# Splitting the 128-row products of an attention and feed-forward kernel over the two halves of TensorE's rows

## The chip, the cores and the metric

The kernel runs on one core of a Trainium2 chip. The metric is the device time of one execution, in microseconds (us); the times of several runs are given by their median. One execution is also recorded by the hardware profiler, and its trace gives the start and the duration of each instruction on each engine.

The engines are TensorE (PE in the profile; its weight loads are PEld), VectorE (DVE), ScalarE (ACT), GpSimd (POOL), and SyncE (SP), which here only issues transfers. TensorE multiplies a stationary operand (the weights, up to 128 rows by 128 columns) with a moving one, and writes or adds the result into a bank of PSUM. The rows are the contracted dimension. A product that contracts over only 64 rows can sit on the lower or the upper half of the rows. In the names used here, T0 is the half of rows 0 to 63 and T1 that of rows 64 to 127.

## What is computed

A block-sparse attention over 4 batches and 8 heads of 768 positions with 64 numbers each, and then a feed-forward layer of 512 to 1024 to 512 with a SoLU and a layer norm, on 3072 tokens:

```python
scores = scale * np.matmul(q, k.transpose(0, 1, 3, 2))
# mask: neighbouring blocks of 32, first and last block, three sampled blocks
scores = np.where(mask, scores, -1000000000.0)
attn = np.exp(scores - max); attn = attn / attn.sum()
x = np.matmul(attn, v)           # heads side by side: 3072 x 512
h = x @ w_in                     # 3072 x 1024
e = np.exp(h - max); solu = h * e / e.sum()
ln = (solu - mean) / np.sqrt(var + 1e-6) * g_ln
out = ln @ w_out                 # 3072 x 512, float32
```

## The kernel before

**Passes and units.** The 768 queries of a batch are taken 256 at a time, so there are 12 passes (four batches by three). A pass has 12 units: four pairs of heads by three parts of the keys (256 keys each). There are 144 units. A unit s does the following:
- `scores(s)`: for two heads and two chunks of 128 keys, the scores are built transposed (keys on the partitions) in a PSUM tile of two banks, `sco`, one bank for each head. There are two such tiles. Each head contracts over 64 rows, head 0 on T0 and head 1 on T1, so the eight products of a unit (four of K times Q, four that add the mask) are 64 rows by 256 columns and come in pairs, T0 and T1 in turn.
- `exps(s)`: one exponential of ScalarE over the 128 x 1024 scores gives `exs`.
- `outs(s)`: eight products with `exs` as weights and the values `VA` (64 numbers and a one, so 65 columns) as the moving operand, contracted over 128 keys, add into `op`. After the third unit of a pair of heads, `normalise` divides by the sum in `op` and writes `xb`.

**The layer.** A pass of 256 queries gives two tiles of 128 tokens. Their x is turned by a transposing transfer (`x_turn`; in the first and the last pass by TensorE). `h_mms` makes h in two PSUM banks: for each half of the 1024 columns four products of 128 rows by 512 columns. `e_exp` takes the exponential of the whole tile on ScalarE, with the sum; `solu` multiplies on VectorE; `ln_turn` turns the result by a transfer; `stats` and `rstd` make the factor of the norm; `o_mms` adds eight products of 128 rows by 512 columns into the one bank `o`, and `store` scales that and sends it out.

**The order.** Nothing is ordered by the compiler. Each step is put on a list with a time in units, `at(when, function, ...)`; the list is sorted by that time (ties in the order of listing), and each engine gets its instructions in this order. So these times set an order, not a clock. A unit s has its exponential at s, the scores of s+2 at s+0.8 and its `outs` at s plus `PV[u]`, u being the part of the keys. `layer_h` and `layer_o` put the layer of a pass into the pass after it and the one after that: h of a tile begins at hs, which is 5 or 11 units into the next pass, and o at hs+9. E = 144 is the end of the last unit and L the number of the last pass; the layer of the last two passes is listed by hand around E, and what is listed after E forms the tail: the x turn of pass L (`x_turn_pe`, at E+0.2), then its h, exponentials, turns, o and stores. Transfers of q, k and v for the next batch are issued on SP from `LD` units apart; GpSimd casts them to bf16, and SP turns q and k.

PSUM is full: two tiles of two banks for the scores, one bank for `op`, two for h, one for `o`. A step that writes a bank anew waits until the one before it has been read. The tile framework adds the semaphores for that.

## Time and profile before

| | |
|---|---|
| median of 3 runs | 234.2 us (233.92 to 234.36) |
| profiled execution, whole | 235.73 us |
| span of its trace | 234.2 us |
| TensorE busy | 223.3 us, 2809 products |
| ScalarE busy | 176.6 us |
| VectorE busy | 128.6 us |
| GpSimd busy | 63.1 us |
| granted clock of TensorE | 1.00 |

The span runs from the first to the last recorded instruction of the profiled execution. Products are pipelined: the next one starts before the one ahead of it has ended, so the busy time of one product is longer than its step in a row of them. In the rows of the timeline, the columns are the start, the time from there to the last end, the engine, the line of the kernel, the operation, the tiles out<-in with the shapes, and the number of instructions that were merged into the row; in brackets the idle time ahead of the row and what ended it. In the table by stages, each engine's busy time is followed by its number of instructions, then come the granted clock, the share of the transfer engines and their GB/s.

### The profile page before, as it was taken

How to read it: one execution, taken by the hardware profiler on the slowest of the kernel's cores; microseconds unless marked ns; L12 is line 12 of the kernel's file. 1: busy time of each engine (PE TensorE's matmuls, PEld its weight loads, DVE VectorE, ACT ScalarE, POOL GpSimd, SP SyncE). 2: the span in 40 equal slices, each digit the busy share in tenths (PEclk: the TensorE clock that was granted, in tenths of full speed). 3: DMA queues.
4: the chain of work that ended last, by engine and by line, in shares of the span. 5: the costliest groups of instructions: out<-in, count | busy, mean ns of one | idle time of the engine just before them, and what ended most of it. 6: DMA issues, size and time to landing. Idle time of an engine off the chain costs nothing.

```text
span 234.2 us, 6717 instructions
## 1 busy us (share of the span) xinstructions
PE 223.3 (95%) x2809; PEld 126.0 (54%) x2809; DVE 128.6 (55%) x318; ACT 176.6 (75%) x206; POOL 63.1 (27%) x101
## 2 busy tenths in 40 slices
PE   5799998999999999999999999999999999989993
PEld 1376655655655555555555555555555555445452
DVE  4344426956356356456456556546556555574783
ACT  4389787679779778878877877867877877786362
POOL 6890493332123224130052133130000000000001
PEclk9999999999999999999999999999999999999999
DMA  5999978797997999992797999974623603702512
GB/s 178 374 325 257 357 263 168 163 249 178 168 270 158 196 268 185 302 204 48 212 206 166 240 238 234 222 196 61 159 11 80 145 4 99 127 4 45 171 56 98
DMA packets 70662, 41.51 MB, mean 177 GB/s; under 512 B 53604, under 2 KB 67428, under 8 KB 70628
## 3 DMA queue, kind: packets, MB, share of 16 engines
q1 hardware_dynamic: 68900, 39.34, 72.0%
q0 software_dynamic: 528, 1.05, 2.4%
q10 hardware_dynamic: 1200, 0.66, 0.9%
q8 instruction: 23, 0.38, 0.7%
q14 instruction: 11, 0.09, 0.1%
HBM read 23.07 MB, written 6.29 MB: 125 GB/s over the span
## 4 chain that ended last, share of the span: by engine, by line
PE 91%; DVE 4%; DMA 1%; issue 1%; ACT 0%; SPq 0%; ACTq 0%; DVEq 0%
PE sco L403 32%; PE h L474 19%; PE op L424 18%; PE o L552 17%; PE tp_q L367 1%; DMA samp_i<-in_sampled_blocks_dram 1%; DVE stats L527 1%; PE oo L552 1%; PE mean_ps L755 1%; PE o_last L559 1%; DVE acc L655 1%; DVE solu L488 1%; PE tpx L457 0%; PE tp_k L367 0%; PE warm L675 0%
## 5 line engine op out<-in xcount | busy, mean ns | idle before, releaser
L411 ACT ACTIVATE exs<-sco 128x1024 bf16<-128x1024 f32 x144 | 144.2, 1023 | 34.8 <-PE sco L403 31.1
L403 PE MATMUL sco<-QT,KT 64*128 64x256 bf16 x576 | 57.1, 277 | 0.3 <-DVE KT L323 0.3
L424 PEld LDWEIGHTS <-exs 128*128 128x128 bf16 x1152 | 44.7, 97 | 20.6 <-issue 10.6
L403 PE MATMUL sco<-mrow,sel 64*128 64x256 bf16 x576 | 55.7, 272 | 0.0
L424 PE MATMUL op<-VA,exs 128*128 128x65 bf16 x1152 | 52.4, 194 | 0.0
L474 PE MATMUL h<-w_in_sb,xT 128*128 128x512 bf16 x192 | 49.5, 380 | 1.7 <-DVE solu L488 0.7
L552 PE MATMUL o<-w_cen_sb,lnT 128*128 128x512 bf16 x176 | 48.3, 381 | 0.0
L488 DVE TENSOR_TENSOR solu<-h,e 128x1024 bf16<-128x1024 f32 (+1 forms) x26 | 29.5, 1140 | 31.8 <-ACT e L481 31.8
L541 POOL TENSOR_TENSOR rstd<-vpe,mhalf 128x1 f32<-128x1 f32 x24 | 13.2, 552 | 121.3 <-DVE vpe L535 111.3
L437 DVE RECIPROCAL recip_all<-op 128x4 f32<-128x4 f32 x48 | 8.7, 182 | 53.0 <-PE op L424 53.0
L403 PEld LDWEIGHTS <-KT 64*128 64x128 bf16 x576 | 18.3, 94 | 33.3 <-issue 29.0
L481 ACT ACTIVATE e<-h 128x1024 bf16<-128x1024 f32 x24 | 24.6, 1024 | 9.9 <-PE h L474 9.9
L527 DVE BATCH_NORM_STATS2 stats<-solu 128x6 f32<-128x512 bf16 x48 | 30.6, 679 | 0.0
L403 PEld LDWEIGHTS <-sel 64*128 64x128 bf16 x576 | 28.4, 95 | 3.7
L474 PEld LDWEIGHTS <-xT 128*128 128x128 bf16 x192 | 15.2, 98 | 18.3 <-issue 4.2
L552 PEld LDWEIGHTS <-lnT 128*128 128x128 bf16 x184 | 13.3, 97 | 15.6 <-issue 8.2
L438 DVE TENSOR_TENSOR xb<-op,recip_all 128x256 bf16<-128x256 f32 x48 | 20.4, 424 | 1.7
L323 POOL CAST n_q<-st_q 128x768 bf16<-128x768 f32 (+2 forms) x19 | 13.5, 720 | 27.2 <-DMA st_q<-in_q_dram 25.9
L323 POOL CAST n_k<-st_k 128x768 bf16<-128x768 f32 x15 | 12.5, 832 | 15.3 <-DMA st_k<-in_k_dram 15.3
L578 DVE TENSOR_SCALAR ot<-o,rstd 128x512 f32<-128x512 f32 x20 | 15.0, 750 | 2.3 <-PE o L552 2.3
L323 POOL CAST VA<-st_v 128x768 bf16<-128x768 f32 x16 | 13.3, 828 | 1.3 <-DMA st_v<-in_v_dram 0.7
L675 PE MATMUL warm<-zero 128*128 128x512 bf16 x8 | 3.8, 627 | 1.9 <-DVE stat_m L613 1.9
(74 smaller groups left out, 85.7 us busy)
## 6 DMA issues: line engine op xcount, KB each, us to landing
st_v<-in_v_dram SPq DMA_DIRECT2D x16, 384.0 KB, 5.5
st_k<-in_k_dram SPq DMA_DIRECT2D x15, 384.0 KB, 4.6
out_dram<-ot SPq DMA_DIRECT2D x10, 512.0 KB, 4.1
st_q<-in_q_dram SPq DMA_DIRECT2D x12, 384.0 KB, 5.0
wf<-in_moe_w_out_dram SPq DMA_DIRECT2D x4, 512.0 KB, 13.5
st_q<-in_q_dram SPq DMA_DIRECT2D x4, 256.0 KB, 5.9
w_in_sb<-in_moe_w_in_dram POOLq DMA_DIRECT2D x1, 1024.0 KB, 13.2
out_dram<-ot SPq DMA_DIRECT2D x3, 256.0 KB, 2.0
```

The costliest lines, as they stand in the source:

```text
L323: eng.tensor_copy(out=out, in_=in_)
L403: nc.tensor.matmul(sco[:, hh, kk * QW : (kk + 1) * QW], kt, qt, start=(m == kk == 0), stop=(m == kk == 1), skip_group_check=True)
L411: nc.scalar.activation(out=exs_of[ps, pr][:, u].rearrange("p a b c -> p (a b c)"), in_=sco_of.pop(s).rearrange("p a b -> p (a b)"), func=A ...
L424: nc.tensor.matmul(op[:, hh, ic, :], exs[:, u, hh, kk, ic * TQ : (ic + 1) * TQ], VA[b % 2][:, 2 * pr + hh, 2 * u + kk, :], start=(u == 0 a ...
L438: nc.vector.tensor_tensor(out=xb_of[ps][:, :, 2 * pr * D : 2 * (pr + 1) * D].rearrange("p c (h d) -> p h c d", h=2), in0=op[:, :, :, 0:D], ...
L474: nc.tensor.matmul(h_of[ps, i][:, half, :], xT, w_in_sb[:, c, half * HF : (half + 1) * HF], start=(c == 0), stop=(c == KD - 1))
L481: nc.scalar.activation(out=e_of[ps, i], in_=h_of[ps, i].rearrange("p a b -> p (a b)"), func=ACT.Exp, scale=1.0, accum_out=esum_all[:, t : ...
L488: nc.vector.tensor_mul(out=solu_of[ps, i][:, a * HF : z * HF], in0=h_of[ps, i][:, a:z].rearrange("p a b -> p (a b)"), in1=e_of[ps, i][:, a ...
L527: nc.vector.bn_stats(out=st[:, half, :], in_=so[:, half * HF : (half + 1) * HF])
L541: nc.gpsimd.tensor_tensor(out=rstd_of[ps, i], in0=stat_of.pop((ps, i)), in1=mhalf, op=ALU.pow)
L552: nc.tensor.matmul(ops_of[ps, i], lhs, w_cen_sb[:, c, :], start=(c == 0), stop=(c == KF - 1))
L578: eng.tensor_scalar(out=o, in0=i, scalar1=rs, scalar2=None, op0=ALU.mult)
```

## The change

All products of the steady passes become products of 64 rows. `outs(s, t)` does the part of half t of a unit's products, eight of them, with 64 of the 128 keys each; the eight of T0 and the eight of T1 are listed at different times (`PV0`, `PV1`), and both add into the same `op`. `h_one` and `o_one` do one half product of h or o each; sixteen of each make a tile. They are listed by slots: eight slots for each half in three units (`T0_AT`, `T1_AT`), which h and o share (`H_AT`, `O_AT`). h takes its T0 halves first, then its T1 halves; o the other way round. `half_mm` keeps the last product on each accumulator, and where a product of the other half is to follow, it puts an empty TensorE instruction ahead of it that waits for that last product.

h now stands in two tiles of one bank each, and its exponential and the product after it are done by halves of the columns (`e_half`, `solu_half`), with one more small sum. h begins at 6 or 12 units into the next pass and spreads over more than 6 units, o begins 12 units after h. What would be listed past the end is drawn in to E by `min`: the h of tile (L-1, 1) and the o of tile (L-2, 1) are now listed as a whole just after E, ahead of `x_turn_pe`. Loads of the later batches are 2.6 units apart for 2.2, the x turn is at 1.65 for 0.6, `rstd` is later within its tile. The layer of the last pass keeps its 128-row products. The table of shifts that is added to `at` is empty, and `turn_pe` and `o_mms` only name the two h banks apart; both are left out here.

```diff
--- before.py
+++ after.py
@@ -241,14 +241,32 @@
     WARM = 6
     FILL = 2
-    PV = (2.55, 1.6, 0.9)
+    SC_AT = 0.8
+    PV0 = (2.2, 1.38, 1.1)
+    PV1 = (3.45, 2.5, 1.55)
+    T0_AT = (1.15, 1.32, 1.5, 1.67, 2.57, 3.28, 3.46, 3.63)
+    T1_AT = (1.36, 1.53, 1.71, 2.23, 2.4, 2.58, 3.1, 3.28)
+    R0, R1 = 2, 0
+    NORM_AT = 0.45
+    ST_AT = 0.2
+    def slot(t, n):
+        return 3 * (n // 8) + (T0_AT, T1_AT)[t][n % 8]
+    H_AT = [[slot(0, n - R0) for n in range(8)], [slot(1, n + 8 + R1) for n in range(8)]]
+    O_AT = [[slot(0, n + 8 - R0) for n in range(8)], [slot(1, n + R1) for n in range(8)]]
+    E_PARTS = ((5.5, 5.6), (6.6, 6.9))
+    HS = 6
+    HS_L = 6
+    O_LAG = 12
     E_AT = 2.95
     HF_AT = ((0, 3, 0.1), (3, 6, 1.1), (6, 8, 1.7))
     OF_AT = ((0, 4, 0.1), (4, 6, 1.1), (6, 8, 2.1))
     L1 = 8
     L2 = 2
-    LD = (2.2, 2.2, 2.2)
+    LD = (2.2, 2.6, 2.6)
     HL = 0.5
     PW = 13.0
     PS = 0.9
@@ -257,12 +275,12 @@
     TP_AT = {(1, 0, 'k'): 23.2, (1, 0, 'q'): 24.2}
     XP_AT = {0: 2.2}
     LP_AT = {}
-    X_AT = 0.6
+    X_AT = 1.65
     X0_AT = 2.2
     W_IN = 4.0
     W_OUT = 7.5
     W_ST = 2.0
-    RS_AT = 2.9
+    RS_AT = 1.9
     nc.scalar.preload_act_table_set("natural_log_exp_and_others")
@@ -272,6 +290,7 @@
     n_r, n_e = NPASS * NP * 4, n_tiles
     recip_all = const_pool.tile([TQ, n_r], FP32)
     esum_all = const_pool.tile([128, n_tiles], FP32)
+    eh_all = const_pool.tile([128, n_tiles, 2], FP32)
     okr = const_pool.tile([128, n_r + n_e], FP32)
     n_ok = const_pool.tile([128, 3], FP32)
     bad = const_pool.tile([128, 1], FP32)
@@ -306,10 +325,39 @@
     p_h = work.enter_context(tc.tile_pool(name="p_h", bufs=1, space=bass.MemoryType.PSUM))
     p_o = work.enter_context(tc.tile_pool(name="p_o", bufs=1, space=bass.MemoryType.PSUM))
+    SYNC = mybir.DependencyInfo(mybir.DependencyClass.Sync, mybir.DependencyReason.DATA)
+    held = {}
+    def half_mm(bank, t, out, lhsT, rhs, start, stop):
+        if bank in held and held[bank][0] != t:
+            nop = nc.tensor.nop()
+            tc.add_manual_dep(nop.ins, held[bank][1], SYNC, reason="one half at a time")
+        i = nc.tensor.matmul(out, lhsT, rhs, start=start, stop=stop, skip_group_check=True)
+        held[bank] = (t, i.ins.name)
     plan = []
...
@@ -412,20 +458,21 @@
             out=exs_of[ps, pr][:, u].rearrange("p a b c -> p (a b c)"),
             in_=sco_of.pop(s).rearrange("p a b -> p (a b)"), func=ACT.Exp, scale=scale)
-    def outs(s):
+    def outs(s, t):
         ps, b, j, pr, u = unit(s)
-        if u == 0:
+        if u == t == 0:
             op_of[ps, pr] = p_op.tile([TQ, 2, PC, D + 1], FP32, tag="op", name=f"op{s}")
         op, exs = op_of[ps, pr], exs_of[ps, pr]
+        r = slice(t * D, (t + 1) * D)
         n = 0
         for hh in range(2):
             for ic in range(PC):
                 for kk in range(2):
-                    nc.tensor.matmul(
-                        op[:, hh, ic, :], exs[:, u, hh, kk, ic * TQ : (ic + 1) * TQ],
-                        VA[b % 2][:, 2 * pr + hh, 2 * u + kk, :],
-                        start=(u == 0 and n == 0), stop=(u == UP - 1 and n == 4 * PC - 1),
-                        skip_group_check=True)
+                    half_mm(("op", ps, pr), t, op[:, hh, ic, :],
+                            exs[r, u, hh, kk, ic * TQ : (ic + 1) * TQ],
+                            VA[b % 2][r, 2 * pr + hh, 2 * u + kk, :],
+                            start=(t == u == n == 0),
+                            stop=(t == 1 and u == UP - 1 and n == 4 * PC - 1))
                     n += 1
     def normalise(ps, pr):
@@ -465,15 +512,57 @@
     def h_mms(ps, i, n0, n1, pool=None):
         if n0 == 0:
             if pool is None:
-                h_of[ps, i] = p_h.tile([128, 2, HF], FP32, tag="h", name=f"h{ps}_{i}")
+                h_of[ps, i] = [p_h.tile([128, HF], FP32, tag=f"h{a}", name=f"h{ps}_{i}_{a}")
+                               for a in range(2)]
             else:
                 h_of[ps, i] = p_sco.tile([128, 2, HF], FP32, tag="sco", name=f"h{ps}_{i}")
         for n in range(n0, n1):
             half, c = divmod(n, KD)
-            xT = xT_of[ps][i][:, c, :] if isinstance(xT_of[ps], list) else xT_of[ps][:, i * KD + c, :]
-            nc.tensor.matmul(h_of[ps, i][:, half, :], xT,
+            h = h_of[ps, i]
+            nc.tensor.matmul(h[half] if isinstance(h, list) else h[:, half, :],
+                             x_chunk(ps, i, c),
                              w_in_sb[:, c, half * HF : (half + 1) * HF],
                              start=(c == 0), stop=(c == KD - 1))
+    def x_chunk(ps, i, c):
+        x = xT_of[ps]
+        return x[i][:, c, :] if isinstance(x, list) else x[:, i * KD + c, :]
+    def h_one(ps, i, t, n):
+        half, c = divmod(n, KD)
+        if t == c == 0:
+            h_of.setdefault((ps, i), []).append(
+                p_h.tile([128, HF], FP32, tag=f"h{half}", name=f"h{ps}_{i}_{half}"))
+        r = slice(t * 64, (t + 1) * 64)
+        half_mm(("h", ps, i, half), t, h_of[ps, i][half], x_chunk(ps, i, c)[r],
+                w_in_sb[r, c, half * HF : (half + 1) * HF],
+                start=(t == 0 and c == 0), stop=(t == 1 and c == KD - 1))
+    def o_one(ps, i, t, c):
+        if t == 1 and c == 0:
+            ops_of[ps, i] = p_o.tile([128, d_model], FP32, tag="o", name=f"o{ps}_{i}")
+        r = slice(t * 64, (t + 1) * 64)
+        half_mm(("o", ps, i), t, ops_of[ps, i], lnT_of[ps, i][r, c, :], w_cen_sb[r, c, :],
+                start=(t == 1 and c == 0), stop=(t == 0 and c == KF - 1))
+    def e_half(ps, i, half):
+        t = ps * PC + i
+        if half == 0:
+            e_of[ps, i] = mo_sb.tile([128, d_ff], BF16, tag="e", name=f"e{t}")
+        nc.scalar.activation(out=e_of[ps, i][:, half * HF : (half + 1) * HF],
+                             in_=h_of[ps, i][half], func=ACT.Exp, scale=1.0,
+                             accum_out=eh_all[:, t, half : half + 1])
+    def solu_half(ps, i, half):
+        t = ps * PC + i
+        if half == 0:
+            solu_of[ps, i] = mo_sb.tile([128, d_ff], BF16, tag="solu", name=f"solu{t}")
+        c = slice(half * HF, (half + 1) * HF)
+        nc.vector.tensor_mul(out=solu_of[ps, i][:, c], in0=h_of[ps, i][half],
+                             in1=e_of[ps, i][:, c])
+        if half == 1:
+            nc.vector.tensor_add(out=esum_all[:, t : t + 1], in0=eh_all[:, t, 0:1],
+                                 in1=eh_all[:, t, 1:2])
     def e_exp(ps, i):
         t = ps * PC + i
...
@@ -773,15 +862,16 @@
         n_units = NPASS * SLOTS
+        E = n_units
         for s in range(n_units):
             at(s, exps, s)
             if s + 2 < n_units:
-                at(s + 0.8, scores, s + 2)
+                at(s + SC_AT, scores, s + 2)
             ps, b, j, pr, u = unit(s)
-            at(s + PV[u], outs, s)
+            at(min(s + PV0[u], E + 0.005), outs, s, 0)
+            at(min(s + PV1[u], E + 0.01), outs, s, 1)
             if u == UP - 1:
-                at(s + PV[u] + 0.02, normalise, ps, pr)
-
+                at(min(s + PV1[u] + NORM_AT, E + 0.02), normalise, ps, pr)
         LQ = nc.sync
         for b in range(1, B):
@@ -801,50 +891,48 @@
                     n += 1
-        def layer_h(ps, i, hs, rs=None):
-            for n0, n1, dt in HF_AT:
-                at(hs + dt, h_mms, ps, i, n0, n1)
-            at(hs + E_AT, e_exp, ps, i)
-            at(hs + E_AT + 0.95, solu, ps, i)
-            if ps * PC + i in LP_AT:
-                at(hs + LP_AT[ps * PC + i], ln_turn_one, ps, i)
-            else:
-                at(hs + E_AT + 0.97, ln_turn, ps, i)
-            at(hs + E_AT + 1.05, stats, ps, i)
-            at(hs + E_AT + (rs or RS_AT), rstd, ps, i)
+        def layer_h(ps, i, hs):
+            for t in range(2):
+                for n in range(8):
+                    at(min(hs + H_AT[t][n], E - 0.6), h_one, ps, i, t, n)
+            for half, (te, ts) in enumerate(E_PARTS):
+                at(min(hs + te, E - 0.3), e_half, ps, i, half)
+                at(min(hs + ts, E - 0.2), solu_half, ps, i, half)
+            at(min(hs + E_PARTS[1][1] + 0.02, E - 0.1), ln_turn, ps, i)
+            at(min(hs + E_PARTS[1][1] + 0.1, E + 0.2), stats, ps, i)
+            at(min(hs + E_PARTS[1][1] + RS_AT, E + 0.21), rstd, ps, i)
         def layer_o(ps, i, os):
-            for n0, n1, dt in OF_AT:
-                at(os + dt, o_mms, ps, i, n0, n1)
-            at(os + OF_AT[-1][2] + 0.8, store, ps, i)
-
-        E = n_units
+            for t in (1, 0):
+                for n in range(8):
+                    at(min(os + O_AT[t][n], E + 0.01), o_one, ps, i, t, n)
+            at(min(os + O_AT[0][7] + ST_AT, E + 0.015), store, ps, i)
         L = NPASS - 1
         for ps in range(L):
             b0 = SLOTS * (ps + 1)
             at(b0 + XP_AT.get(ps, X_AT), x_turn_pe if ps in XP_AT else x_turn, ps)
             for i in range(PC):
                 t = ps * PC + i
-                hs = b0 + 5 + 6 * i
-                if t < 2 * L - 2:
+                hs = b0 + (HS if ps < L - 1 else HS_L) + 6 * i
+                if t < 2 * L - 1:
                     layer_h(ps, i, hs)
-                if t < 2 * L - 4:
-                    layer_o(ps, i, hs + 9)
-
-        at(E - 10.9, o_mms, L - 2, 0, 0, 4)
-        at(E - 9.9, o_mms, L - 2, 0, 4, 8)
-        at(E - 9.1, store, L - 2, 0)
-        layer_h(L - 1, 0, E - 8.5)
-        for n0, n1, dt in HF_AT:
-            at(E - 5 + dt + HL, h_mms, L - 1, 1, n0, n1)
-        at(E - 5 + HL + E_AT, e_exp, L - 1, 1)
-        at(E - 5 + HL + E_AT + 0.95, solu, L - 1, 1)
-        at(E - 5 + HL + E_AT + 0.97, ln_turn, L - 1, 1)
+                if t < 2 * L - 3:
+                    layer_o(ps, i, hs + O_LAG)
+        hs = SLOTS * L + HS_L + 6
+        for t in range(2):
+            for n in range(8):
+                at(min(hs + H_AT[t][n], E + 0.02), h_one, L - 1, 1, t, n)
+        for half in range(2):
+            at(E + 0.03, e_half, L - 1, 1, half)
+            at(E + 0.04, solu_half, L - 1, 1, half)
+        at(E + 0.05, ln_turn, L - 1, 1)
         at(E + 0.25, stats, L - 1, 1)
         at(E + 0.26, rstd, L - 1, 1)
-        at(E - 5.9, o_mms, L - 2, 1, 0, 3)
-        at(E - 1.9, o_mms, L - 2, 1, 3, 8)
-        at(E - 0.95, store, L - 2, 1)
+        for t in (1, 0):
+            for n in range(8):
+                at(E + 0.021, o_one, L - 2, 1, t, n)
+        at(E + 0.06, store, L - 2, 1)
         at(E + 0.1, o_mms, L - 1, 0, 0, 8)
         at(E + 0.2, x_turn_pe, L)
         at(E + 0.3, store, L - 1, 0, A)
```

25 lines of the change are left out of this document (19 added, 6 removed).

## The prediction

> **What bounds the kernel now.** I read the page first: its busy line, then the chain that ended last.
>
> ```profile
> PE 223.3 (95%) x2809; PEld 126.0 (54%) x2809; DVE 128.6 (55%) x318; ACT 176.6 (75%) x206; POOL 63.1 (27%) x101
> PE 91%; DVE 4%; DMA 1%; issue 1%; ACT 0%; SPq 0%; ACTq 0%; DVEq 0%
> ```
>
> TensorE (PE) is busy 95% and carries 91% of the chain, so a unit takes as long as its products. ScalarE, next, has a quarter of the span free. I then cut the span at the starts of exps 0, 12, 24, 36, 132 and 143, first all engines, then the exps alone (last line).
>
> ```profile
> 0.00:9.18 9.18, 5.68 (x23) 1.77 (x24) 4.17 (x17) 2.98 (x5) 7.17 (x22) 1.00 0.77 249
> 9.18:23.26 14.08, 13.77 (x210) 9.41 (x210) 5.69 (x16) 11.73 (x12) 8.02 (x12) 1.00 1.10 306
> 23.26:39.35 16.09, 15.57 (x228) 9.69 (x226) 6.84 (x18) 12.76 (x15) 9.38 (x13) 1.00 0.87 262
> 39.35:57.84 18.49, 17.69 (x236) 10.19 (x234) 13.96 (x35) 14.08 (x17) 6.14 (x8) 1.00 0.89 203
> 57.84:196.66 138.82, 138.32 (x1793) 77.69 (x1792) 75.69 (x177) 112.65 (x129) 29.06 (x41) 1.00 0.81 171
> 196.66:215.62 18.96, 18.28 (x223) 9.54 (x222) 10.47 (x26) 14.05 (x17) 1.65 (x3) 1.00 0.34 71
> 215.62:234.24 18.62, 14.03 (x109) 7.74 (x107) 11.74 (x33) 8.33 (x16) 1.68 (x3) 1.00 0.31 102
> ...
> 57.84:196.66 138.82, 96.44 (x97) 1.00 0.81 171
> ```
>
> The eight steady passes are units 36 to 131 (one of the 97 exps is cut by the edge): 138.82/96 = 1.446 us a unit. The granted clock is 1.00 in every stage. Prices come from the timeline of PE.
>
> ```profile
> 101.55 0.66 PE L424 MATMUL op<-VA,exs 128*128 128x65 bf16 x16
> 102.15 0.39 PE L403 MATMUL sco<-QT,KT 64*128 64x256 bf16 x4
> 102.38 0.38 PE L403 MATMUL sco<-mrow,sel 64*128 64x256 bf16 x4
> 102.69 0.43 PE L424 MATMUL op<-VA,exs 128*128 128x65 bf16 x8
> 102.96 1.24 PE L474 MATMUL h<-w_in_sb,xT 128*128 128x512 bf16 x5
> 104.13 0.39 PE L403 MATMUL sco<-QT,KT 64*128 64x256 bf16 x4
> 104.36 0.38 PE L403 MATMUL sco<-mrow,sel 64*128 64x256 bf16 x4
> 104.58 0.38 PE L403 MATMUL sco<-QT,KT 64*128 64x256 bf16 x4
> ...
> 219.95 3.63 PE L474 MATMUL h<-w_in_sb,xT 128*128 128x512 bf16 x16 [0.52 <-DVE xT L462]
> ```
>
> Four score products of 64 rows start 0.22 us before the next four (104.36 to 104.58): two pairs, one product on each half of the rows, 0.110 us a pair, 0.44 a unit. A product of L424 goes on every 0.031 us, weight load included (16 of them last 0.66; without the last one's own 0.19, 0.47/15). One of 512 columns goes on every 0.216 ((3.63-0.38)/15). A unit has 8 of L424 (0.25) and, with one tile of 8 h and 8 o products in six units, 16/6 of 0.216 (0.576): 1.264 in all. The rest, 0.18, is at the changes between 64 and 128 rows: 16 of L424 from 101.55 are through at 102.05, the scores begin at 102.15; they are through at 102.60, L424 begins at 102.69; five of h are through at 104.04, the scores begin at 104.13. So 0.09 to 0.10 at each change, nearly two in a unit.
>
> **What the change does to a steady unit.** All products become 64-row ones, so these changes vanish: at best 1.446 becomes 1.264. But each L424, h and o product is now two, at the same length: a product's time goes by its columns, as the 64-row scores show, and the number of rows buys nothing. The halves' work is 3 x 0.44 + 3 x 0.248 + 8 x 0.216 = 3.79 us per three units on each side, and 1.264 is reached only if neither half ever stands still. So what counts is how PE takes products off one list. The pairs of scores start a few ns apart and in the listed order, and no row shows a product starting ahead of one listed before it; all these pairs are of equal length, so how a long one stands beside short ones isn't shown. I take the likeliest: a product whose half is busy holds up all those behind it. Then the listing of three units (T0 and T1 are the halves, P a block of eight L424 halves, 0.248 us, its last start at 0.217; H a half of h or o, 0.216) gives, from each group of scores to the next:
> - T0 T0 T1 T0 T1 T0 T1, all H: four T0 in a row, the last T1 starts with the last T0: 0.867.
> - P0 H1 P0 H1 H0 H1: the first H1 starts at 0.22, after the block's last issue; the second P0 runs 0.248 to 0.496, the second H1 starts 0.468, H0 0.496, the last H1 0.684 to 0.900. T0 is free at 0.712, but the pairs of scores need both: 0.900.
> - P0 H1 H0 H1 P1 H0 P1 P1 H0: H1 0.220 and 0.436, the first P1 0.652 (last issue 0.869), H0 0.872, the P1s 0.900 and 1.148 (last issue 1.365), the last H0 1.368 to 1.584: 1.584. Here T0 waits 0.4 us at one stretch for the issue of T1's blocks.
> With three groups of scores (1.32), less 0.11 where T0 leaves the skewed second group early, 4.56 us, 1.520 a unit: the 0.18 saved is paid back with 0.256 of standing halves. Bounds: 1.264 if the halves never wait, 1.65 if besides nothing may end before what was listed ahead of it (same walk).
>
> [...]
>
> The added waits: at each change of half in one accumulator an empty PE instruction waits for the other half's last product, and all that is listed behind stands. For op that product comes 0.43 us earlier in the walk, for o also 0.43, for h over a unit. It can be waited for about 0.2 us after its last column.
>
> ```profile
> 102.80 1.02 ACT L411 ACTIVATE exs<-sco 128x1024 bf16<-128x1024 f32 x1 [0.75 <-PE sco L403]
> ```
>
> (The last pair of scores starts at 102.49 and is through at 102.60, the exp starts 102.80.) 0.216 + 0.2 = 0.42 against 0.43: nothing in the steady passes, 0.05 a unit if a wait itself costs 0.1 us.
>
> The other engines and the h banks:
>
> ```profile
> L411 ACT ACTIVATE exs<-sco 128x1024 bf16<-128x1024 f32 x144 | 144.2, 1023 | 34.8 <-PE sco L403 31.1
> L481 ACT ACTIVATION_READ_ACCUMULATOR e<-h 128x1 f32 x24 | 4.7, 195 | 0.0
> L488 DVE TENSOR_TENSOR solu<-h,e 128x512 bf16<-128x512 f32 x4 | 2.6, 686 | 1.7 <-ACT e L481 1.7
> L576 ACT ACTIVATE ot<-o,rstd 128x512 f32<-128x512 f32 x2 | 1.4, 690 | 0.3 <-PE o L552 0.3
> lnT<-solu SPq DMA_TRANSPOSE x22, 3.7
> xT<-xb SPq DMA_TRANSPOSE x10, 3.8
> ```
>
> A tile's exp in two halves is some 2 x 0.69 (the 512-wide row) and two reads, overlapped in part: 1.2 to 1.7 us in six units, so ScalarE has at most 1.023 + 0.28 = 1.30 a unit, under 1.52. An h bank, before free for three units, now has from its last half product to the next tile's first 1.23 units (5.23 to 6.46 in the listing), 1.87 us at 1.52; product 0.22, completion 0.2, exp 0.69 + 0.1, solu 0.69, signals 0.1: 2.0 and up to 0.3 for an exp in the way. The 0.1 to 0.4 that is late falls on T0, which then stands 0.4 for P1 anyway; I take nothing, up to 0.05 a unit. The later x turn (1.65 for 0.6) is covered: h starts at 6 for 5, 4.35 units later, over 6 us for the 3.8. lnT has its 3.7 in over five units before o. Loads 2.6 units apart, casts and turns behind them on SP and POOL, end near unit 71 for a batch that begins at 72 and needs its last pair at 81.
>
> **The ends.** Passes 0 to 2 (48.66 us) have few or no o products. There a P0 and a P1 hardly overlap: 24 x 0.031 = 0.74 more per three units against two to four changes of 0.1 saved; transposes keep the others. Pass 0 +1.5, pass 1 +0.5, pass 2 (o later, from unit 31) -1.0: +1.0 in all, -3 to +4. The last eleven units go by the steady price: 16.7 for 18.96, as work is put off to the end. There:
>
> ```profile
> 216.02 1.11 PE L424 MATMUL op<-VA,exs 128*128 128x65 bf16 x24
> 217.09 1.89 PE L552 MATMUL o<-w_cen_sb,lnT 128*128 128x512 bf16 x8
> 218.82 0.61 PE L457 MATMUL tpx<-ident,xb 128*128 128x128 bf16 x8
> ...
> L578 DVE TENSOR_SCALAR ot<-o,rstd 128x512 f32<-128x512 f32 x20 | 15.0, 750 | 2.3 <-PE o L552 2.3
> ```
>
> Before, between the last L424 and the last pass's x turn (tpx), from which h, exp, transposes, o and store follow, stand 8 products, 1.73 us. After, there stand ahead of tpx: h of tile (L-1,1) as eight T0 and then eight T1, o of (L-2,1) as eight T1 and then eight T0. In runs of one half, with an accumulator change between, nothing overlaps: 32 x 0.216 = 6.91 (6.05 at best). Then o's one bank must be scaled and freed before (L-1,0)'s eight: 0.2 + 0.75 + 0.05 = 1.0, before covered by the 24 of L424. So tpx comes 7.9 us later (5 if the halves overlap as far as the waits let them). After the last exp there now come one P0 and three P1 blocks for one block of 8 before: 24 x 0.031 = 0.74, less 0.14 that the 24 of L424 took anyway, +0.6. The tail: 18.62 + 8.5 = 27.1.
>
> **Sum:** 9.18 + 48.66 + 1.0 + 96 x 1.520 (145.9) + 16.7 + 27.1 = 248.5 us of span for 234.24. The profiled execution took 235.73, 1.5 more than its span; the median of the runs, 234.2, equals the span, so the same +14.3 on the median gives 248.5.
>
> **Rivals.** (a) Each half has its own queue, deep enough that no order holds it: the list is balanced for this, 3.79 us of work on each half in three units, which speaks for it; no row shows it. PE would go to 1.264. Then the h bank decides: 1.23 x 1.264 = 1.55 us allowed for the 2.0 to 2.3 needed, 0.65 late in six units: 1.37. 9.18 + 47.2 + 96 x 1.37 (131.5) + 15.1 + 26.5 = 229.5, faster; if that cover holds (half exps of 0.5), 1.30 and 222. It decides as soon as a half can hold about eight waiting products. [...]
> (b) A few products can wait at a half (two to four): by the same walk 1.41 to 1.48 with the banks: 236 to 244, I say 240.
> (c) Ends in order too: 1.65: 9.18 + 50.7 + 158.4 + 18.2 + 27.5 = 264. Against it: halves are separate accumulators and banks.
> That the split does nothing is excluded: it removes each 128-row product of these passes.
>
> **How the numbers follow.** The forecast's case has 0.54 (own range 243 to 254: banks, waits and early passes), (a) 0.25, (b) 0.13, (c) 0.08. 225 to 256 holds nearly all of the first, (b) and two thirds of (a): about 0.8. A run of this kernel can tell 0.2% (0.5 us) from no change. Faster: (a), 0.25. Within 0.2%: 0.02, from the low end of (b). Slower: 0.73.
>
> **What would show it.** Per unit: exps 1.52 us apart in the steady stage; in PE's timeline no gap of 0.09 between scores and others; T0 products waiting behind blocks of L424 on the other half, PE busy still near its share. In the tail: 7 us of h and o products between the last L424 and tpx. Wrong: exps 1.26 to 1.40 apart, and L424 halves that run beside an h half listed behind them; or a tail that grows by less than 5 us.

## The result, and the profile after

The kernel after the change takes 248.99 us (median of 4 runs, 248.39 to 250.39), the kernel before beside it 234.28 (233.92 to 234.63): 1.0636 times as long, 95% interval 1.0589 to 1.0684. The profiled execution took 248.39, its span is 246.7. 248.5 was predicted.

The page of the kernel after, busy line and chain:

```profile
PE 233.5 (95%) x4297; PEld 181.6 (74%) x4297; DVE 131.7 (53%) x362; ACT 178.4 (72%) x250; POOL 63.5 (26%) x101
PE 83%; DVE 5%; DMA 5%; ACT 3%; POOL 1%; issue 1%; SPq 1%; DVEq 0%; ACTq 0%
```

TensorE is as busy as before (95%), with half as many products again, but the chain is on it for 83% and not 91%: the share of the others is the first hint that an end of the program has grown. The span cut at the same events as before (the starts of exps 0, 12, 24, 36, 132 and 143), all engines, kernel after:

```profile
0.00:7.54 7.54, 4.83 (x23) 1.62 (x24) 3.57 (x17) 2.98 (x5) 5.52 (x19) 1.00 0.67 211
7.54:22.77 15.23, 14.40 (x286) 11.17 (x286) 6.03 (x16) 11.79 (x13) 9.77 (x15) 1.00 1.10 317
22.77:42.88 20.11, 19.69 (x362) 14.03 (x359) 6.37 (x17) 12.45 (x15) 10.96 (x15) 1.00 0.81 253
42.88:60.20 17.32, 17.32 (x339) 13.75 (x334) 10.81 (x31) 14.26 (x22) 4.63 (x6) 1.00 0.87 169
60.20:200.78 140.58, 139.95 (x2820) 116.96 (x2816) 78.67 (x208) 113.31 (x163) 29.27 (x41) 1.00 0.83 169
200.78:215.98 15.20, 15.20 (x317) 12.69 (x313) 10.43 (x29) 12.54 (x20) 1.10 (x2) 1.00 0.49 88
215.98:246.67 30.69, 22.14 (x176) 11.41 (x171) 15.86 (x45) 11.06 (x22) 2.23 (x4) 0.96 0.24 71
```

Against the same rows of before, in us: start -1.64, passes 0 to 2 +4.00 (+1.15, +4.02, -1.17), the 96 steady units +1.76 (1.446 to 1.464 a unit), the last eleven units -3.76, and behind the last exp +12.07 (18.62 to 30.69); +12.43 in all. The steady passes, for which the change is made, are nearly even. The loss is at the ends, above all in the last row. (Its granted clock of 0.96 comes from after the last product: it is 1.00 up to 243 us and 0.67 behind that.)

That row, in PE's timeline of the kernel after:

```profile
219.09 2.98 PE L337 MATMUL h<-w_in_sb,xT 64*128 64x512 bf16 x16
221.91 3.85 PE L337 MATMUL o<-w_cen_sb,lnT 64*128 64x512 bf16 x16
226.67 1.89 PE L641 MATMUL o<-w_cen_sb,lnT 128*128 128x512 bf16 x8 [0.92 <-DVE ot L667]
228.40 0.61 PE L504 MATMUL tpx<-ident,xb 128*128 128x128 bf16 x8
229.52 3.63 PE L522 MATMUL h<-w_in_sb,xT 128*128 128x512 bf16 x16 [0.52 <-DVE xT L509]
```

Sixteen halves of h, sixteen of o, a wait of 0.92 for the o bank and eight whole products stand ahead of the last pass's x turn (tpx), where before eight whole products stood. The turn comes 12.42 us after the last exp's start, 228.40 - 215.98; before 3.20 (218.82 - 215.62). That is 9.2 of the 12.07. The other 2.86 lie at the very end: from the issue of the last transfer to the end of the span it is 6.19 us for 3.33. The branch that ends the program, by its line, in the kernel before and in the kernel after (ns; at us):

```profile
L917 PEldq COMPARE_BRANCH  x1: 353/353/353, 231.5 to 231.5; - x1
```

```profile
L1005 PEldq COMPARE_BRANCH  x1: 4458/4458/4458, 241.1 to 241.1; - x1
```

The same instruction on PE's queue takes 4.46 us for 0.35. The other engines' last events by this line lie at 242.2 or earlier. The transfers of the kernel after between 241.1 and 245.5 us have this row among them (queue and kind: packets, MB, share of the transfer engines):

```profile
q8 instruction: 1, 0.02, 3.0%
```

It is one block of 16 KB, from 242.08 to 244.18 us. In the kernel before no such block lies within the branch; the last one ahead of it landed at 225.80.

Last, PE's timeline in a steady unit, kernel after:

```profile
112.78 0.27 PE L449 MATMUL sco<-mrow,sel 64*128 64x256 bf16 x2
112.89 0.19 PE L337 MATMUL op<-VA,exs 64*128 64x65 bf16 x1
112.89 0.27 PE L449 MATMUL sco<-mrow,sel 64*128 64x256 bf16 x1
112.92 0.29 PE L337 MATMUL op<-VA,exs 64*128 64x65 bf16 x4
113.02 0.39 PE L337 MATMUL h<-w_in_sb,xT 64*128 64x512 bf16 x1
113.04 0.25 PE L337 MATMUL op<-VA,exs 64*128 64x65 bf16 x3
113.14 0.37 PE L337 MATMUL o<-w_cen_sb,lnT 64*128 64x512 bf16 x1
```

This settles what the prediction could only assume. `outs` lists its eight halves in one piece, so the h half, on the other half of the rows, is listed behind all eight. It starts at 113.02, after five of them, and three start after it. The steady stage has 128 places where a half of h or o starts within a block of eight, and in each of them three are left. (In the rest of the trace there are 31 more: three are left in 28, and four, two and one in one each.) So in the steady stage TensorE neither held everything behind a block whose half was busy nor let a half of h or o start ahead of all eight: it went past three in each of the 128 places. I call this the window of three; it is a count of these starts, and what sets it was not shown. The first op half starts together with a score (112.89), so the gap of 0.09 between scores and others is gone, as predicted.

### The profile page after: what moved, and what is told of

Same layout as the page of the kernel before. It is cut to its first block, busy times and chain, and to the rows that moved or that the text cites. A ratio compares the mean times of both kernels' runs of the same rounds, so it can differ in the third digit from the quotient of the medians.

```text
span 246.7 us, 9766 instructions
## 1 busy us (share of the span) xinstructions
PE 233.5 (95%) x4297; PEld 181.6 (74%) x4297; DVE 131.7 (53%) x362; ACT 178.4 (72%) x250; POOL 63.5 (26%) x101
## 3 DMA queue, kind: packets, MB, share of 16 engines
HBM read 23.07 MB, written 6.29 MB: 119 GB/s over the span
## 4 chain that ended last, share of the span: by engine, by line
PE 83%; DVE 5%; DMA 5%; ACT 3%; POOL 1%; issue 1%; SPq 1%; DVEq 0%; ACTq 0%
PE op L337 24%; PE sco L449 24%; PE h L337 17%; PE o L337 12%; DMA xT<-xb 2%; DMA st_k<-in_k_dram 2%; PE h L522 1%; DVE stats L616 1%; ACT exs L457 1%; ACT e L552 1%; PE mean_ps L844 1%; PE tp_q L413 1%; PE o L641 1%; POOL n_k L371 1%; DVE solu L561 1%
## 5 line engine op out<-in xcount | busy, mean ns | idle before, releaser
L337 PE MATMUL h<-w_in_sb,xT 64*128 64x512 bf16 x352 | 103.7, 378 | 0.4 <-DMA xT<-xb 0.4
L337 PEld LDWEIGHTS <-exs 64*128 64x128 bf16 x2304 | 89.6, 94 | 13.4 <-PE op L337 4.2
L337 PE MATMUL o<-w_cen_sb,lnT 64*128 64x512 bf16 x320 | 98.2, 379 | 0.1
L337 PE MATMUL op<-VA,exs 64*128 64x65 bf16 x2304 | 97.2, 190 | 0.6 <-DVE xb L485 0.2
L449 PE MATMUL sco<-mrow,sel 64*128 64x256 bf16 x576 | 73.2, 269 | 0.0
L561 DVE TENSOR_TENSOR solu<-h,e 128x512 bf16<-128x512 f32 x44 | 30.4, 692 | 48.8 <-ACT e L552 46.3
L449 PEld LDWEIGHTS <-KT 64*128 64x128 bf16 x576 | 42.8, 94 | 11.6 <-issue 1.1
L552 ACT ACTIVATE e<-h 128x512 bf16<-128x512 f32 x44 | 26.3, 598 | 15.7 <-PE h L337 15.7
L337 PEld LDWEIGHTS <-xT 64*128 64x128 bf16 x352 | 30.2, 93 | 6.4 <-DMA xT<-xb 0.6
L337 PEld LDWEIGHTS <-lnT 64*128 64x128 bf16 x320 | 25.8, 94 | 5.7 <-PE o L337 0.6
```

What stands on the lines that cost most here:

```text
L337: i = nc.tensor.matmul(out, lhsT, rhs, start=start, stop=stop, skip_group_check=True)
L449: nc.tensor.matmul(sco[:, hh, kk * QW : (kk + 1) * QW], kt, qt, start=(m == kk == 0), stop=(m == kk == 1), skip_group_check=True)
L552: nc.scalar.activation(out=e_of[ps, i][:, half * HF : (half + 1) * HF], in_=h_of[ps, i][half], func=ACT.Exp, scale=1.0, accum_out=eh_all[: ...
L561: nc.vector.tensor_mul(out=solu_of[ps, i][:, c], in0=h_of[ps, i][half], in1=e_of[ps, i][:, c])
```

## The experiments

What was to be told apart. My theory after the result: three separate things, a window of three in the steady units (so a finer mix of the list gains), 9.2 us of products and waits that the new list puts ahead of tpx, and 2.9 us of a branch whose price has nothing to do with the change's products. The rivals: the steady unit is bound by something other than the order of the list, such as the exchange of the h banks (then mixing it gains nothing); the tail is bound by the o bank and its scaling, not by the products; the long branch comes with the split.

All but the last start from the kernel after. Four were run together (the kernel before beside them 235.51, 232.83 to 236.23, 7 runs), then four more on another chip (before 235.08, 234.58 to 236.39, 11 runs). Stages come from the one profiled execution of each.

Early and late starts have to be kept apart: with one and the same list the first exp starts at 7.54 (e1_pad) or at 9.18 to 9.20 (e2_singles, e3_tailpairs), and pass 0 then takes 1.0 us longer (e6_tail starts between, at 8.49). So the early stages are compared between runs with the same start.

**e1_pad: the branch moved by 64 instructions.** Four of the warming products give way to 36 short ones. The question is whether the branch's 4.46 us go by how many instructions stand ahead of it or come with the longer program.

```
-        fill(WARM)
+        fill(WARM - 4)
+        for _ in range(36):
+            nc.tensor.matmul(warm[:, 0, 0:48], zero[:, 0:128], zero[:, 0:48], start=True, stop=True)
```

> The changed kernel with 64 more TensorE instructions at its start: 4 of the 6 long warming products are replaced by 36 short ones of 48 columns (about the same time there), nothing else. In the trace of the changed kernel the branch at the end takes TensorE 4.46 us (0.35 before), and a block of 16 KB of instructions is fetched only while it waits. [...] Theory B (a program with 50% more TensorE instructions always pays for its branch): still over 4 us, time as the changed kernel's, 249.0.

Measured 246.97 (245.84 to 248.73), 1.0545 times before (1.0439 to 1.0651). The branch in it:

```profile
L1007 PEldq COMPARE_BRANCH  x1: 353/353/353, 240.9 to 240.9; - x1
```

It is back at 0.35, and the end behind the last transfer at 3.33 (after: 6.19), -2.86. All the other stages agree with those of the kernel after within 0.2 us. The times alone (246.97 and 248.99) have overlapping intervals; the stage decides. All further variants keep these or like short products.

**e2_singles: the P blocks mixed in one by one.** e1_pad, and each block of eight halves of op is listed as eight single products among the h and o halves, 0.0245 units apart (`outs` is given the number of the product); the normalising step follows the last.

```
-            at(min(s + PV0[u], E + 0.005), outs, s, 0)
-            at(min(s + PV1[u], E + 0.01), outs, s, 1)
+            for n in range(8):
+                at(min(s + PV0[u] + 0.0245 * n, E + 0.005), outs, s, 0, n)
+            for n in range(8):
+                at(min(s + PV1[u] + 0.0245 * n, E + 0.01), outs, s, 1, n)
```

> As e1_pad, and the eight products of a block of outs on one half are listed one by one, 0.0245 units apart, in place of eight in a row; the same products, slots and waits. Theory A (PE starts a product past at most three blocked ones, so blocks of eight and long halves hold each other up): walking the list with that window of three gives 1.39 us a unit for 1.45, so 6 to 7 us less than e1_pad over 107 units. Theory B (the exchange of the h banks, exp and solu set the 1.45): no change against e1_pad. Theory C (no look past blocked products at all): the walk gives about 1.40 here too, but 1.52 for the blocks, which the changed kernel did not show.

Measured 242.15, 1.0337 (1.0236 to 1.0438), 4.8 us under e1_pad (6 to 7 were expected). Its steady stage, 96 units:

```profile
62.31:198.15 135.84, 133.44 (x2821) 113.74 (x2817) 78.80 (x208) 115.01 (x162) 29.35 (x41) 1.00 0.87 177
```

1.415 a unit; its undisturbed passes run at 1.387 where those of e1_pad and of the kernel after run at 1.453 (starts of exps twelve apart). Walking the list, that is following it product by product, with a window of three had given 1.39. With the same products, engines and banks, only the order has changed, so the order set a part of the unit. The size alone does not show the window: the walk without any look past a waiting product had given 1.40 for this list. It had given 1.52 for the blocks, and there 1.453 was measured; together with the starts shown above this speaks for the window. What keeps the mean above 1.387 is in part another thing, x turns that now come late. PE's waits in the steady passes of this kernel:

```profile
PE h L337 <- DMA xT<-xb: 2.1, 2, 1.2
PE op L337 <- DVE xb L486: 0.3, 1, 0.3
```

**e3_tailpairs: h and o halves of the tail in turn.** e1_pad, and behind the last unit the h halves of (L-1,1) and the o halves of (L-2,1) alternate, so that both halves of the rows work.

```
-        for t in range(2):
-            for n in range(8):
-                at(min(hs + H_AT[t][n], E + 0.02), h_one, L - 1, 1, t, n)
+        for n in range(8):
+            at(E + 0.02 + 0.0002 * n, h_one, L - 1, 1, 0, n)
+            at(E + 0.0201 + 0.0002 * n, o_one, L - 2, 1, 1, n)
+            at(E + 0.022 + 0.0002 * n, h_one, L - 1, 1, 1, n)
+            at(E + 0.0225 + 0.0002 * n, o_one, L - 2, 1, 0, n)
...
-        for t in (1, 0):
-            for n in range(8):
-                at(E + 0.021, o_one, L - 2, 1, t, n)
```

> As e1_pad, with the 32 half products after the end of the last unit listed in pairs: h of T0 with o of T1 in turn, then h of T1 with o of T0, in place of four runs of eight on one half. Theory A (PE's list ahead of the last x turn sets the end): the 6.3 us from the first of them to the last become some 3.7, and the whole is 2.5 to 3.2 us shorter than e1_pad. Theory B (the end waits for exps, solu and transfers of those tiles anyway): no change.

Measured 248.16, 1.0552 (1.0448 to 1.0656): not faster than e1_pad, and exp 143 to tpx grew from 12.42 to 13.51. PE's timeline, its waits behind the last units, and the cut of that stretch in this kernel:

```profile
228.56 3.57 PE L641 MATMUL o<-w_cen_sb,lnT 128*128 128x512 bf16 x8 [2.00 <-DVE ot L667]
```

```profile
PE o L641 <- DVE ot L667: 2.0, 1, 2.0
PE o L337 <- DVE ot L667: 0.8, 1, 0.8
```

```profile
226.60:228.50 1.90, 0.00 (x0) 0.00 (x0) 1.73 (x5) 0.46 (x2) 0.00 (x0) 1.00 0.00 0
228.50:232.20 3.70, 3.64 (x13) 1.43 (x13) 1.60 (x6) 0.00 (x0) 0.55 (x1) 0.54 0.73 213
```

The pairs did save products: 4.9 us with their wait for the 6.5 of the kernel after. But PE then stood 0.82 and 2.00 us for the one o bank (0.92 in the kernel after), with VectorE busy 1.73 of 1.90, and when it went on, the granted clock was 0.54: the eight products took 3.57 for 1.89. Theory B's "no change" met the number, but not by its reason: the forecast had neither the longer wait nor the clock. The rival that names the o bank has its point.

**e4_whole: whole products for the first 18 units.** e1_pad, with the op products of units 0 to 17 as before the change (`outs_whole` is the old `outs`).

```
+            if s < 18:
+                at(s + (2.55, 1.6, 0.9)[u], outs_whole, s)
+                if u == UP - 1:
+                    at(s + 0.92, normalise, ps, pr)
+                continue
```

> As e1_pad, with units 0 to 17 done with whole 128-row products of outs, at the listing times of the kernel before; all later units as in the changed kernel. Theory A (in the first units nothing runs beside the blocks of eight, so the split adds 0.75 us for three units there): units 3 to 15 take 12.3 us for 15.3, the whole is 3 us shorter than e1_pad. Theory B (loads and casts set the pace of the first passes): no change, or units 18 to 24 give it back.

Measured 246.42, 1.0495 (1.0394 to 1.0596). Passes 0 and 1 of this kernel, and then of e3_tailpairs, which begins with the split list and has the same start:

```profile
9.20:22.80 13.60, 13.18 (x211) 9.02 (x211) 5.88 (x16) 11.74 (x13) 8.04 (x12) 1.00 1.10 308
22.80:41.36 18.56, 18.05 (x293) 11.64 (x290) 6.49 (x17) 12.45 (x16) 10.99 (x15) 1.00 0.87 268
```

```profile
9.18:25.25 16.07, 15.64 (x286) 12.11 (x286) 5.97 (x16) 11.79 (x13) 8.65 (x13) 1.00 1.10 303
25.25:45.27 20.02, 19.60 (x362) 13.96 (x359) 6.37 (x17) 12.46 (x16) 10.36 (x15) 1.00 0.68 214
```

32.16 us for 36.09, and 0.34 given back in pass 2: -3.6. This is the price of a split without work for the other half, in units 3 to 15 0.60 us per three units (14.81 us in e3_tailpairs, 12.40 here). Of the total little shows, since its branch took 3.90 us and its end 5.62 for 3.33: with 144 products fewer ahead of it (504 for the 648 of e3_tailpairs in these two passes) the branch is long again.

**e5_r0: the T0 half one slot later.** e2_singles, and the h and o halves of T0 begin one slot ahead of the others instead of two.

```
-    R0, R1 = 2, 0
+    R0, R1 = 1, 0
```

> As e2_singles (1.387 us a unit in its steady passes), and T0's share of the slots is moved on by one place (R0 = 1 for 2), so that the next tile's first T0 half of h, and the first T0 half of o after its T1 halves, come one slot later. Theory A (what is left above 1.264 is waiting at the exchange of the h banks and at the change of half in o's bank): the walk with both gives 1.35, that is 3 to 4 us less than e2_singles. Theory B (what is left is the order of the products on the two halves): no change or worse, 1.39 to 1.41.

Measured 240.69, 1.0225 (1.0181 to 1.0269), against 242.15 for e2_singles. The intervals overlap, so the stages decide. Steady units 1.397 for 1.415, in undisturbed passes 1.37 for 1.387 (1.35 expected). The direction is that of theory A, the size half. What was waited for shows in the trace, at one exchange of an h bank in the kernel after (the product that empties the bank, and the next tile's first half into it):

```profile
113.01 0.69 DVE L561 TENSOR_TENSOR solu<-h,e 128x512 bf16<-128x512 f32 x1 [2.29 <-ACT e L552]
113.75 0.37 PE L337 MATMUL h<-w_in_sb,xT 64*128 64x512 bf16 x1
```

The half starts 0.05 us after VectorE has read the bank (113.70). In the kernel after it is so for 16 of the 17 tiles whose h begins between 61 and 202 us, and in e2_singles for all but two. In e5_r0 the first bank has been free for 0.39 us or more each time, while the second is mostly still taken 0.05 us after it is read. So the exchange is waited for, and with one of its two waits gone the unit is 0.02 us shorter. In the profiled execution the tail lost most of the gain, by accident: there the clock fell again, to 0.51, and exp 143 to tpx took 14.05 for 12.19.

```profile
222.00:224.50 2.50, 2.50 (x7) 0.85 (x7) 0.60 (x4) 0.00 (x0) 0.55 (x1) 0.51 0.46 185
```

**e6_tail: the turn ahead of the o halves' second part.** e1_pad; h of T0 and o of T1 are paired, then comes the x turn, then the other pairs; the store of (L-2,1) comes ahead of the h tile's products on VectorE; (L-1,0)'s whole o products go behind the last pass's first h products, where their bank is free.

```
+        for n in range(8):
+            at(E + 0.02 + 0.0002 * n, h_one, L - 1, 1, 0, n)
+            at(E + 0.0209 + 0.0002 * n, o_one, L - 2, 1, 1, n)
+            at(E + 0.0231 + 0.0002 * n, h_one, L - 1, 1, 1, n)
+            at(E + 0.0232 + 0.0002 * n, o_one, L - 2, 1, 0, n)
+        at(E + 0.0229, x_turn_pe, L)
...
+        at(E + 0.029, store, L - 2, 1)
+        at(E + 0.35, o_mms, L - 1, 0, 0, 8)
+        at(E + 0.55, store, L - 1, 0, A)
```

> As e1_pad, with the products after the last unit relisted: four h halves on T0 alone (cover for o's bank), four pairs of h T0 and o T1, four o T1 alone, then the last x turn, then eight pairs of h T1 and o T0; the store of tile (L-2,1) ahead of the exponential's products on VectorE; o of (L-1,0) only after the h of the last pass's first tile. e3_tailpairs showed that pairing alone saves 1.7 us of products but then stands 2.0 us for o's bank, and that the clock halves for the next eight products. Theory A (the list ahead of the x turn and these two waits are the tail): from the last exp to the last transfer's issue 24.5 us become 20 to 21.5, the whole 3 to 4.5 us under e1_pad. Theory B (the chain from the x turn to the end sets it, and o of (L-1,0) now falls into it): under 1.5 us gained.

Measured 244.50, 1.0398 (1.0367 to 1.0429), 2.5 under e1_pad, between the two forecasts. PE's timeline:

```profile
222.90 1.24 PE L337 MATMUL o<-w_cen_sb,lnT 64*128 64x512 bf16 x5
224.07 0.62 PE L504 MATMUL tpx<-ident,xb 128*128 128x128 bf16 x8
...
226.68 1.67 PE L522 MATMUL h<-w_in_sb,xT 128*128 128x512 bf16 x7 [0.16 <-issue]
228.19 1.89 PE L641 MATMUL o<-w_cen_sb,lnT 128*128 128x512 bf16 x8
```

The turn comes 6.12 us after the last exp for 12.42, but the last transfer is issued 15.47 behind it for 12.09: 21.6 for 24.5 together, -2.9. Both causes hold: 6.3 us of products and waiting stood ahead of the turn, and half of them have to be done behind it anyway.

**e7_all: all of these together.** Singles, R0 = 1, whole products for units 0 to 17, e6_tail's list, and 53 short products that are to keep the branch short.

> All of it: products of outs listed one by one, R0 = 1, units 0 to 17 with whole products, the relisted tail, and a TensorE program whose end falls where the branch is short. Theory A (window, banks, tail and early units are independent terms): 234.2 us of span before, less 96 x 0.097 in the steady passes, less some 4 in the last eleven units, plus 8 to 9 in the tail, early passes -1 to 0: 228 to 231, that is 2% to 1% under the kernel before. Theory B (the terms hide one another): 234 to 238, no gain over the kernel before.

Measured 233.08 (230.62 to 234.03, 6 runs), 0.9892 times before (0.9854 to 0.9931): 1.1% under the kernel before, little but clear of the interval, and well under the kernel after. The same cuts, from pass 0 on:

```profile
9.17:22.62 13.45, 13.01 (x210) 8.95 (x210) 5.87 (x16) 11.69 (x12) 8.37 (x13) 1.00 1.10 304
22.62:40.95 18.33, 17.81 (x289) 11.68 (x288) 6.27 (x17) 12.44 (x15) 10.18 (x15) 1.00 0.85 258
40.95:57.44 16.49, 16.49 (x340) 13.01 (x336) 10.98 (x31) 14.15 (x22) 5.41 (x7) 1.00 1.00 202
57.44:192.32 134.88, 132.57 (x2820) 111.45 (x2816) 79.34 (x208) 114.46 (x162) 29.18 (x41) 1.00 0.85 176
192.32:206.84 14.52, 14.52 (x321) 12.11 (x318) 10.23 (x29) 12.71 (x19) 1.10 (x2) 1.00 0.49 93
206.84:231.56 24.72, 20.27 (x176) 10.69 (x173) 15.73 (x45) 11.07 (x22) 2.23 (x4) 1.00 0.30 88
```

Against before: -0.4 in passes 0 to 2, -3.9 in the steady units (1.405), -4.4 in the last eleven, +6.1 behind the last exp; the start is the same. The 228 to 231 us that were expected are a span; the spans of the six runs are 228.8 to 232.2, that of this execution 231.56, so the upper edge was met. The terms came out otherwise: the steady units were to give 9.3 and gave 3.9, and the tail was to cost 8 to 9 and cost 6.1. Five of the eight steady passes still run at 1.41 to 1.45, where the others run at 1.37 to 1.38; why was not taken apart.

**e8_before_branch: the kernel before, with 160 instructions more on PE.** Six of its warming products become 86 of 24 columns, so that the branch stands at another place in PE's count of instructions and little else changes. The question is whether that place makes it long in this kernel too.

```
-        fill(WARM)
+        fill(WARM - 6)
+        for _ in range(86):
+            nc.tensor.matmul(warm[:, 0, 0:24], zero[:, 0:128], zero[:, 0:24], start=True, stop=True)
```

> [...] Theory A (the stall of the branch is a matter of that place alone): the branch takes over 3 us and the end from the last transfer's issue grows from 3.3 to about 6.2 us; whole 2 to 3 us longer than the kernel before. Theory B (it needs the longer program): 0.35 us, no change.

Measured 236.79, 1.0069 (1.0035 to 1.0102), and the branch:

```profile
L919 PEldq COMPARE_BRANCH  x1: 3773/3773/3773, 231.6 to 231.6; - x1
```

The end grew from 3.33 to 5.50, and the median is 1.7 us above that of the kernel before beside it (2 to 3 were expected). So the kernel before can be made to pay it too, and the kernel after freed of it (e1_pad): in these kernels it goes not with the split but with how many instructions stand ahead of the branch (64 more: 4458 to 353 ns; 160 more: 353 to 3773).

## Why the prediction was right, and where its steps were not

The total was right (248.5 for 248.99); its likeliest case was not. Term by term, in us of the profiled span:
- **Start:** 9.18 predicted, 7.54 measured. Not from the change: kernels with the same list start either way.
- **Passes 0 to 2:** 49.66 predicted, 52.66 measured; with the late start, which the kernel before has too, 53.40 (e3_tailpairs), 4.7 over the 48.66 before and beyond the upper end of +4. The failed term is the net price of P blocks without a partner, and how far it reaches. I set "two to four changes of 0.1 saved" against 0.74 per three units, which gave +1.5 for pass 0, and then only +0.5 and -1.0. Units 0 to 18 took 24.40 us in e3_tailpairs, 21.37 before and 20.88 with whole products (e4_whole): +3.0, or 0.5 per three units, and whole products take all of it away. The other 1.7 lie in units 18 to 36 (29.00 for 27.29), which e4_whole splits too, and were not taken apart. The +4.02 of pass 1 is not the price of that pass: its units 21 to 24 take 7.11 us for 3.97, but units 24 to 27, behind the cut, 3.92 for 6.29.
- **Steady units:** 1.520 predicted, 1.464 measured, 140.6 for 145.9. The failed step is "a product whose half is busy holds up all those behind it". Three are overtaken in each of the 128 places of the steady stage. This is rival (b), "two to four products can wait at a half", which had 1.41 to 1.48 and 0.13 of the chance; (a), 1.37, and (c), 1.65, are out. That nothing ends ahead of what was listed before it, the premise of (c)'s 1.65, no run shows; 1.464 a unit was measured. Of the two signs that I had named under "Wrong", one is in the trace, op halves beside an h half listed behind them (112.92 to 113.04); the other, exps 1.26 to 1.40 apart, is not. The forecast's consequence, that T0 waits behind blocks of the other half, held in a weaker form, as e2_singles shows by taking it away.
- **The covers taken as free:** nearly right in price. PE's waits in the steady passes of the kernel after name no bank and no change of half; they are

```profile
PE h L337 <- DMA xT<-xb: 0.4, 1, 0.4
PE op L337 <- DVE xb L485: 0.2, 1, 0.2
```

But this view has only stretches in which PE as a whole stands, and a half that stands beside a working one is not in it. The h banks are waited for at nearly every tile, as the rows under e5_r0 show: from the last half product into a bank to the next tile's first it takes 1.88 us (111.87 to 113.75), where the prediction had 2.0 and more, its 0.1 for signals being an estimate (0.05 from VectorE's read to the half, 113.70 to 113.75), and the listing leaves 1.23 units, 1.79 us at 1.453. The part of this that e5_r0 takes away goes with 0.02 us a unit, within the 0.05 that were allowed. What the changes of half cost was not shown.

- **Last eleven units:** 16.7 predicted, 15.20 measured; the same error of the unit's price.
- **Tail:** tpx 8.5 us later predicted, 9.2 measured: 6.5 us of h and o halves without overlap (6.91 predicted), 1.1 for the o bank (1.0), of which PE stands 0.92, and 1.6 more from the last exp to the first of those halves (0.6). In this last stretch, 3.11 us for 1.47, stand 48 op halves, six blocks where four were counted, with some halves of h and o between them. The growth behind tpx that I took as nothing up to the last transfer is nothing (12.09 both times).
- **The end:** 2.86 for the branch, for which the prediction had no term; it was put at nothing.

The errors: -1.6 at the start, +3.0 early, -5.3 in the steady units, -1.5 in the last eleven, +0.7 and +2.9 at the end: -1.8 in all, 246.67 for 248.5 of span. The median came out at 248.99, 2.3 above the span and not equal to it as in the runs of before: the four runs here take 1.7 to 1.8 us more than their own spans, and the profiled one, 248.39, was the shortest of them. In the kernel before the profiled one took 1.5 us more than its span, and its 235.73 lay above the median. So the number was met by luck: a unit that was too dear and two ends that were too cheap made up for each other. With the measured units and everything else as I had costed it, 241.7 was to be expected (248.5 less 5.3 and 1.5); the missing 7.3 are the early passes (3.0), the branch (2.9), the median's distance to the span (2.3) and the tail (0.7), less the start (1.6).

## What to carry to other kernels

Here the split gained only where both halves had work listed within reach: 1.387 us a unit in undisturbed passes with the list mixed finely, 1.453 with blocks of eight, 1.446 before, while in units 3 to 15, without such work, it cost 0.60 us per three units. So list the halves finely in turn, and leave products whole where nothing stands beside them. Even so all of it together gave 1.1%. Cost the ends of the program with the same care as the loop: here the loop was even and the end alone lost 12 us. Look at the duration of the last branch in a profile (0.35 to 4.46 us here) before comparing two kernels within 1%.

## What the runs showed of the hardware

**A window of three.** In the trace of the kernel after, TensorE started a half of h or o ahead of three op halves listed earlier in all 128 places of the steady stage, and mixing the list to suit gave 1.387 us a unit for 1.453 (e2_singles). What sets the three was not shown. On the ends the trace is no witness, as they are modelled, but by the prediction's walk a unit that holds to ends in order would have taken 1.65.

**A branch that takes 0.35 or 3.8 to 4.5 us.** It took 353 ns in the kernel before and in e1_pad, and 4458, 3898 and 3773 in the kernel after, e4_whole and e8_before_branch. 64 instructions more ahead of it made it short in e1_pad, 160 more made it long in e8_before_branch. In the kernel after the block of 16 KB on the instruction queue (q8) starts 1.0 us after the branch and lands 1.4 us before its end; in the kernel before none is under way while the branch lasts. (In both one more block starts 0.7 us behind its end.) So in these kernels the length goes with the instruction count, and in the two traces a transfer of instructions lies within the long branch and none within the short one. Which counts make it long was not shown. The time lost was 2.2 to 2.9 us, less than the branch's length, since the other engines' ends run beside its first part (up to 242.2 in the kernel after, for a branch from 241.1 to 245.6).

**The start of PE.** PE's first products in the kernel before and in the kernel after:

```profile
7.14 1.03 PE L675 MATMUL warm<-zero 128*128 128x512 bf16 x2
8.10 0.61 PE L403 MATMUL sco<-QT,KT 64*128 64x256 bf16 x4
```

```profile
6.35 0.60 PE L764 MATMUL warm<-zero 128*128 128x512 bf16 x2
6.89 0.39 PE L449 MATMUL sco<-QT,KT 64*128 64x256 bf16 x4
```

In the late start the same products run slower (1.03 for 0.60, 0.61 for 0.39). The profile gives a granted clock of 1.00 for both stretches. To the end of pass 0 this makes 2.7 us (25.25 in e3_tailpairs, 22.59 in e1_pad). What decides the start stayed open, as did why the clock fell in the tail of e5_r0 and not in that of the kernel after, with standing times of 0.91 and 0.92 us.
